# Seven products instead of eight for ten gate/up chunks of one row block, with sums and a load placed elsewhere

## The chip, the cores and the metric

The kernel runs on one core of a Trainium2 chip. A core has a matrix engine (TensorE, PE in the profile), three engines for element work (VectorE, DVE; ScalarE, ACT; GpSimd, POOL) and queues for DMA (most transfers here are issued by SyncE, SP). Each engine works through its own instructions in order and waits for others at semaphores. Matrix products land in PSUM, in banks of 512 f32 values per partition; PE and ACT, DVE and PE hand such banks to each other. POOL works on SBUF only in this kernel. The metric is device time in microseconds (us); lower is better.

## The reference

```python
xn = _layernorm(x, axis=-1)                      # x: 2048 x 512
s = _A_ref(xn, A_k_cache, A_v_cache, A_wq, A_wo) # 32 heads, 2048 keys, Dh 128
g = _silu(_B_ref(xn, B_W_gate, B_W_up, B_W_down))
return x + s * g

def _B_ref(x, W_gate, W_up, W_down):             # D 512, F 1792
    gate = jnp.einsum("bsd,df->bsf", x, W_gate)
    up = jnp.einsum("bsd,df->bsf", x, W_up)
    gate = gate * (gate > 0)
    return jnp.einsum("bsf,fd->bsd", gate * up, W_down)
```

The change concerns gate and up of `_B_ref` for one quarter of the rows.

## The kernel before, in words

The 2048 rows are four blocks of 512 (Q = 0 to 3); the 1792 hidden columns are 14 chunks of 128 (fc). PE runs one long program in the order in which the code emits it, and the time before and after the attention's main loop is one stream: block 0's gate/up, its down products, block 2's gate/up, then the attention of 32 heads, into which the rest of the gated unit (blocks 1 and 3, and down for blocks 1 to 3) is mixed piece by piece.

**Block 0.** `head_ln` and `emit_gate_up(0)` (L715) give gate and up from centered rows. Chunk by chunk: four matmuls into a gate bank (L739), four into an up bank (L743), then `finish_gate_up` (L693): ACT takes relu of the gate bank (L699), DVE multiplies with the up bank into hT (L703). Banks come from a ring of three slots of two banks (`ring_acquire`), or are the two banks of ps_acc. After each chunk `ln_task` (L571) does a step of the normalization of all rows: statistics on DVE, a square root on ACT, the normalized rows xn_sb on POOL (L455), then a DMA transpose into xnT (L567). These run per quarter of the rows: four POOL instructions and four transposes each.

**Down products of block 0.** `emit_down` (L829) has four tiles of 14 matmuls (L842), in turn in the two banks of ps_acc. Each is gated: tanh on ACT (L850), then on DVE a TENSOR_SCALAR (L854) and a product with the bank into g_sb (L858), which frees the bank for the tile after next.

**Block 2.** `emit_gate_up(2)` goes through 14 chunks as for block 0, with xnT in place of the centered rows. Between the chunks it emits other work:

- `emit_tx` (L599), eight sums on DVE of the halves of xnT into TX, which overwrites xn_sb and so waits for all transposes (L609 to L617). All later products by halves read TX;
- `emit_wd_scale` (L775, the down weights times a constant, DVE) and `emit_wd_sums` (L780, four sums of the down weights, POOL, L789 to L795);
- `emit_sw(0)` (L656), scaling of the first query weights on ACT and four sums on POOL (L677 to L682);
- `emit_st`, the query products of the first two heads (L924), combined on DVE (L929, with one copy, L938);
- the first three score pairs S0 to S2 (L1626), whose exponentials (L1638) start the attention;
- `emit_hs` (L803), sums of the halves of hT on DVE (L813 to L822), read by the down products of block 2 (`emit_d`, L1239, combined at L1248).

All these "products by halves" follow one scheme: a product of 2 x 2 blocks is made from seven products of sums of blocks instead of eight of the blocks themselves, and the results are added up from PSUM by DVE. In the kernel before, the queries, the down products of blocks 1 to 3 and gate/up of blocks 1 and 3 are made so; gate/up of block 2 is not.

Of the kernel before, what the change touches and what calls it, by code (L numbers as in the profile page):

```python
# [52 lines left out]
def bass_recurrent_scan__mha_block_cached__glu_gated_reglu__prompt_kernel(  # L53
# [63 lines left out]
    with ExitStack() as es:  # L117
# [111 lines left out]

        sem_x = [newsem(16) for _ in range(QB)]  # L230
# [36 lines left out]
        sem_fo = newsem()  # L267
        sem_ft = [[newsem(16) for _ in range(2)] for _ in range(QB - 1)]
# [91 lines left out]
        sem_wd.sig(sp.dma_start(Wd_sb[:], B_W_down.rearrange("(c p) d -> p c d", p=128)))  # L360
# [210 lines left out]
        def ln_task(i):  # L571
            if i < 4 * (QB - 1):
# [4 lines left out]
                if i == 2:  # L577
                    ctok = ln_finish(0)
                    _wait(dve, ctok)
# [76 lines left out]
        def emit_sw(pr):  # L656
# [8 lines left out]
            if pr in (0, 2):  # L665
# [49 lines left out]
        def emit_gate_up(Q):  # L715
            qs = slice(Q * NQ, (Q + 1) * NQ)
            h_tok = None
            for fc in range(FC):
                fs = slice(fc * 128, (fc + 1) * 128)
                if Q == 0 and fc < HFC:  # L720
                    s = half_slots[fc]
                    finish_gate_up(Q, fc, s, half_tok[(fc, 0)], half_tok[(fc, 1)])
                    continue
                if Q == 0 and fc == HFC:
# [5 lines left out]
                if fc == 0:  # L730
                    _wait_all(pe, xt_ready[Q])
                xT, xs = (xcT, slice(0, NQ)) if Q == 0 else (xnT, qs)
                if Q == 0 and fc in FCS:
# [4 lines left out]
                for c in range(DC):  # L738
                    ins = pe.matmul(g_ps, Wg_sb[:, c, fs], xT[:, c, xs],  # L739
                                    start=(c == 0), stop=(c == DC - 1))  # L740
                gtok = sem_gate.sig(ins)
                for c in range(DC):
                    ins = pe.matmul(u_ps, Wu_sb[:, c, fs], xT[:, c, xs],  # L743
                                    start=(c == 0), stop=(c == DC - 1))
                gu_tok = sem_gu.sig(ins)
                h_tok = finish_gate_up(Q, fc, s, gtok, gu_tok)
                if Q == 2:
                    if fc < 4:
                        emit_tx(2 * fc)
                        emit_tx(2 * fc + 1)  # L750
                    elif fc < 6:
                        emit_wd_scale(fc - 4)
                    if fc == 3:
                        emit_sw(0)
                    if fc == 5:
                        for k in range(4):
                            emit_wd_sums(k)
                    if fc in (7, 9):
                        gu_scale((fc - 7) // 2)
                    if 9 <= fc < 12:  # L760
                        emit_M([(emit_st, 2, 0, 0, fc - 9)])
                    elif fc == 12:
                        emit_S_pair(0)
                        emit_M([(emit_st, 1, 0, 0, 3)])
                    elif fc == 13:
                        emit_S_pair(1)
                        emit_M([(emit_st, 2, 0, 1, 0)])
                        emit_S_pair(2)
                        for k in range(4):
                            emit_hs(2, 0, k)  # L770
# [9 lines left out]
        def emit_wd_sums(k):  # L780
# [18 lines left out]
            wd_tok["t"] = t  # L799
# [3 lines left out]
        def emit_hs(Q, part, i):  # L803
# [6 lines left out]
            if i == 0:  # L810
                _wait(dve, h_done[(Q, FC - 1 if part else HF + 3)])
                _wait(dve, d_done.get(Q - 2))
                t = dve.tensor_tensor(s3, a11, a21, ALU.subtract)  # L813
# [15 lines left out]
        def emit_down(Q, h_last_tok):  # L829
            assert Q == 0  # L830
            ytok = None
            for j in range(4):
# [28 lines left out]
                acc_free[jb] = gtok  # L861
            y_last["t"] = ytok

# [3 lines left out]
        emit_down(0, emit_gate_up(0))  # L867
# [1306 lines left out]
```

## Time and profile before

| | |
|---|---|
| median of 3 runs | 1237.11 us (1236.94 to 1237.14) |
| profiled execution | 1237.32 us, of it span 1236.0 us |
| granted TensorE clock | 0.999 |
| block 0, gate/up | 0 to 31.5 us |
| block 0, down | 31.5 to 43.6 us |
| block 2, gate/up, with the head of the attention mixed in from 60.85 | 43.6 to 71.4 us |
| attention | from 68.6 us (first score pair) to the end |

The profile is of one execution. Its rows by stage give the length, then for each engine the busy time and the number of instructions. In a timeline row the first number is the start, the second how long the group took, then engine, line, operation, tile written, tiles read, shapes and count, and in brackets how long the engine had been idle and for whom it waited. Instructions of one engine overlap a little: of matmuls in a row each starts before the one ahead has ended, so durations per instruction are read from starts. The rows by group give the busy total, the mean of one in ns, and the idle time ahead of them.

### The profile page before, as it was taken

What the parts mean: (1) busy time and instruction counts of PE and PEld (TensorE: products, weight loads), DVE (VectorE), ACT (ScalarE), POOL (GpSimd) and SP (SyncE); (2) the same over time, 40 slices, a digit from 0 to 9 for tenths busy, and PEclk for the clock granted to TensorE, in tenths of its full rate; (3) what the DMA queues carried; (4) which work ended last, traced back from release to release, by engine and by line L of the source; (5) the groups of instructions that cost most, each with busy time, mean ns of one, the idle gap of its engine ahead of it and who ended that gap; (6) DMA issues with size and microseconds to landing.
All of it is one profiled execution on the core that took longest, in us unless ns stands there. A gap on an engine that the chain in (4) does not pass through costs nothing.

```text
span 1236.0 us, 29081 instructions
## 1 busy us (share of the span) xinstructions
PE 1219.0 (99%) x11717; PEld 817.2 (66%) x11927; DVE 877.4 (71%) x1324; ACT 1041.5 (84%) x1110; POOL 835.1 (68%) x946
## 2 busy tenths in 40 slices
PE   9999999999999999999999999999999999999998
PEld 5466666776666666666666666666666666666665
DVE  6668787667676767677676767676676767675587
ACT  3457877668889999999999999999999999989994
POOL 3355876313767867787688776986778767668368
PEclk9999999999999999999999999999999999999999
DMA  9712331323222544264614653374524472248616
GB/s 276 158 31 37 77 78 26 52 48 94 53 53 52 141 128 122 49 158 109 174 36 120 142 159 89 84 172 100 154 52 120 113 192 48 53 103 162 126 35 141
DMA packets 285061, 127.21 MB, mean 103 GB/s; under 512 B 253696, under 2 KB 279552, under 8 KB 280064
## 3 DMA queue, kind: packets, MB, share of 16 engines
q1 hardware_dynamic: 283584, 124.55, 43.6%
q8 instruction: 95, 1.56, 0.5%
q10 hardware_dynamic: 1344, 0.79, 0.2%
q14 instruction: 38, 0.31, 0.1%
HBM read 57.93 MB, written 25.17 MB: 67 GB/s over the span
## 4 chain that ended last, share of the span: by engine, by line
PE 96%; ACT 2%; issue 1%; DMA 0%; DVE 0%; SPq 0%
PE ps_acc L1735 37%; PE ps_r L1626 34%; PE ps_r L1060 5%; PE ps_r L1178 3%; PE ps_r L1523 3%; PE ps_r L1239 3%; PE ps_r L924 2%; ACT PT L1638 2%; PE ps_r L743 2%; PE ps_r L739 2%; PE ps_r L1458 2%; PE ps_acc L842 1%; PE ps_r L1767 1%; PE ps_r L1555 1%; PE ps_r L1554 1%
## 5 line engine op out<-in xcount | busy, mean ns | idle before, releaser
L1638 ACT ACTIVATE PT<-ps_r 128x1024 bf16<-128x1024 f32 x1024 | 989.8, 1025 | 128.3 <-PE ps_r L1626 114.1
L1735 PEld LDWEIGHTS ps_acc<-V_sb,PT 128*128 128x128 bf16 x8192 | 545.3, 98 | 226.8 <-issue 28.3
L1735 PE MATMUL ps_acc<-V_sb,PT 128*128 128x129 bf16 x8192 | 630.8, 220 | 1.0
L1626 PE MATMUL ps_r<-QT_sb,KT_sb 128*128 128x512 bf16 x1849 | 555.0, 379 | 10.1 <-ACT PT L1638 0.3
L1065 DVE TENSOR_TENSOR UVR<-UVR,ps_r 128x512 f32<-128x512 f32 (+1 forms) x228 | 168.7, 755 | 78.9 <-PE ps_r L1060 76.5
L1626 PEld LDWEIGHTS ps_r<-QT_sb,KT_sb 128*128 128x128 bf16 x2048 | 163.2, 98 | 30.9 <-ACT PT L1638 1.5
L1389 DVE TENSOR_TENSOR s_acc<-s_acc,ps_r 128x1024 f32<-128x1024 f32 x108 | 131.2, 1219 | 36.4 <-PE ps_r L1555 15.0
L1405 DVE TENSOR_TENSOR s_acc<-s_acc,ps_r 128x512 f32<-128x512 f32 x152 | 101.4, 686 | 26.6 <-PE ps_r L1523 21.4
L1658 DVE TENSOR_TENSOR Onorm<-ps_acc,rz_sb 128x512 bf16<-128x512 f32 x127 | 87.8, 691 | 4.4
L1489 POOL TENSOR_TENSOR TI<-OX 128x512 f16<-128x512 f16 x38 | 43.1, 1156 | 69.7 <-issue 68.1
L1655 DVE RECIPROCAL rz_sb<-ps_acc 128x4 f32<-128x4 f32 x127 | 23.2, 183 | 93.6 <-PE ps_acc L1735 92.7
L1025 POOL TENSOR_TENSOR TI<-xn_sb 128x512 f16<-128x512 f16 x48 | 55.8, 1163 | 38.9 <-PE ps_r L1060 38.9
L1065 DVE TENSOR_TENSOR QT_sb<-UVR,ps_r 128x512 bf16<-128x512 f32 x72 | 49.4, 686 | 37.1 <-PE ps_r L1060 34.8
L1489 POOL TENSOR_TENSOR TI<-OT_store 128x512 f16<-128x512 bf16 (+1 forms) x38 | 43.4, 1165 | 32.4 <-PE ps_r L1523 16.1
L1333 POOL TENSOR_TENSOR WX<-Wo_sb 128x512 f16<-128x512 bf16 x7 | 8.1, 1155 | 84.2 <-DVE Wo_sb L1323 45.3
L1025 POOL TENSOR_TENSOR TI<-xn_sb,TI 128x512 f16<-128x512 f16 x48 | 56.0, 1166 | 0.0
L1025 POOL TENSOR_TENSOR TI<-xnT 128x512 f16<-128x512 bf16 x36 | 41.6, 1157 | 13.8 <-PE ps_r L1060 13.8
L1060 PE MATMUL ps_r<-TI,SI 128*128 128x512 f16 x126 | 47.8, 379 | 0.1
L1523 PE MATMUL ps_r<-TI,SI 128*128 128x512 f16 x114 | 43.2, 379 | 0.0
L1025 POOL TENSOR_TENSOR TI<-xnT,TI 128x512 f16<-128x512 bf16 x36 | 41.6, 1156 | 0.0
L1154 POOL TENSOR_SCALAR gB<-gB 128x512 bf16<-128x512 bf16 x14 | 20.8, 1486 | 30.3 <-DVE gB L1184 30.3
L1133 POOL TENSOR_TENSOR UVR<-UVR,UVR 128x512 f32<-128x512 f32 x24 | 29.8, 1274 | 11.3 <-DVE UVR L1065 11.3
(236 smaller groups left out, 1436.5 us busy)
## 6 DMA issues: line engine op xcount, KB each, us to landing
sums<-s_acc SPq DMA_DIRECT2D x20, 1024.0 KB, 4.5
s_acc<-sums SPq DMA_DIRECT2D x18, 1024.0 KB, 6.2
V_sb<-in_A_v_cache_dram SPq DMA_DIRECT2D x32, 512.0 KB, 4.3
Wq_sb<-in_A_wq_dram SPq DMA_DIRECT2D x16, 256.0 KB, 3.5
Wo_sb<-in_A_wo_dram SPq DMA_DIRECT2D x8, 512.0 KB, 3.8
out_dram<-g_sb SPq DMA_DIRECT2D x4, 512.0 KB, 4.5
KR<-sums SPq DMA_DIRECT2D x4, 512.0 KB, 4.5
OT_store<-Onorm SPq DMA_TRANSPOSE x127, 2.7
```

Of the source, the lines that this page charges most:

```text
L1025: return sem_ui.sig(pool.tensor_tensor(dst, x, y, o))
L1060: return sem_up.sig(pe.matmul(dst, lhs, rhs, start=start, stop=stop, skip_group_check=True))
L1065: dve.tensor_tensor(dst, x, ps, ALU.add))
L1178: ins = pe.matmul(ps_r[:, bank, :], L(i), R(i), start=(i == 0), stop=(i == HC - 1))
L1389: t = sem_opa.sig(dve.tensor_tensor(dst, dst, sb, op))
L1405: t = dve.tensor_tensor(dst, dst, sb, op)
L1489: return sem_oi.sig(pool.tensor_tensor(dst, x, y, o))
L1523: return sem_op.sig(pe.matmul(dst, lhs, rhs, start=start, stop=stop, skip_group_check=True))
L1626: ins = pe.matmul(ps_r[:, 2 * s + tt, :], KT_sb[h % 2][:, t * 128:(t + 1) * 128], QT_sb[qt_slot[(h, Q)]][:], start=True, stop=True)
L1638: act.activation(PT[pb][:], ps_r[:, 2 * s:2 * s + 2, :], ACTF.Exp, scale=scale / WSC)
L1658: dve.tensor_tensor(Onorm[ob][:], o_ap, rz_sb[:].to_broadcast([128, 4, Dh]), ALU.mult))
L1735: ins = pe.matmul(o_ap, PT[pb][:, tt, j * 128:(j + 1) * 128], V_sb[vb][:, t, 0:VW], start=(t == 0 and j % 2 == 0), stop=(t == KT - 1 and j ...
```

## The change

Gate/up of block 2 gets a function of its own. Chunks 0 to 9 are taken in five pairs (t = 0 to 4). For a pair, gate and up weights of 256 columns, halved along the 512 inputs, are the four blocks of one factor; the 512 rows, halved along rows and inputs, are those of the other. Seven products (m) of four matmuls each, 128x256, fill one bank with both chunks. Products 1, 6, 7 and 4 of a pair accumulate in one bank, which ACT copies out after 1, 6 and 7; DVE adds the copies to the banks of products 2, 5 and 3. Half of h comes from DVE, half from POOL (`high`). Chunks 10 to 13 (F10 to F13) stay as they were, cut into pieces that stand between products. The order of products and pieces is a table of slots.

```diff
+        def sgu_scale(t, i):
+            W = (Wg_sb, Wu_sb)[i][:, :, 256 * t:256 * (t + 1)]
+            _wait(act, up0_tok[2 * t + 1])
+            f_tok[("w", t)] = sem_fs.sig(act.activation(W, W, ACTF.Copy, scale=GSC))
+        def sgu_sums(t):
...
+            _wait(pool, f_tok[("w", t)])
+            if t >= 3:
+                _wait(pool, y_last["t"])
+            k = f_tok[("x", t, 0)] = sem_fw.sig(pool.tensor_tensor(X[:, 0], a21, a22, ALU.add))
...
+        def sgu_rows():
...
+            _wait_all(dve, xt_ready[2])
+            k = sem_fx.sig(dve.tensor_tensor(XS[0], b12, b11, ALU.subtract))
...
+                if fc in (6, 7):
+                    sgu_scale(0, fc - 6)
+                if fc == 7:
+                    sgu_sums(0)
+                if fc in (9, 10):
+                    sgu_scale(1, fc - 9)
...
+            A = [ps_acc[:, 0, :], ps_acc[:, 1, :], bk(2 * X)]
+            a_free = [[acc_free[0]], [acc_free[1]], None]
...
+                if m == 1:
+                    _wait_all(pe, [f_tok[("w", t)]] + (ring_tok[X] if t == 2 else a_free[t % 3]) + xt_ready[2])
...
+                elif m == 5:
+                    _wait_all(dve, [p, f_tok[("w1", t)], f_tok.get(("hi", t - 2))])
...
+            def high(t):
+                b = t % 2
+                _wait(act, f_tok[("gh", t)])
+                k = sem_fa.sig(act.activation(hgh[b][:], hgh[b][:], ACTF.Relu))
+                _wait_all(pool, [k, f_tok[("uh", t)]])
+                f_tok[("hi", t)] = f_tok["hi"] = sem_fh.sig(pool.tensor_tensor(
...
+            slots = {7 * t + d: (t, m) for t in range(NSP) for m, d in ((1, 0), (6, 4), (2, 6), (7, 8), (5, 10), (4, 12), (3, 16))}
...
+                if n == 7 * (NSP - 1) + 2:
+                    emit_sw(0)
+                if n == e + 5:
+                    emit_wd_scale(0)
+                if n == e + 9:
+                    emit_wd_scale(1)
+            ring_order[:] = [X, Y, Z]
+            for k in range(4):
+                emit_wd_sums(k)
+            gu_scale(0)
+            emit_M([(emit_st, 2, 0, 0, 0)])
...
         def emit_down(Q, h_last_tok):
+            for i in range(2):
+                sgu_scale(2, i)
...
+                if j < 2:
+                    for i in range(2):
+                        sgu_scale(3 + j, i)
+                    sgu_sums(1 + j)
+                if j == 0:
+                    sgu_rows()
+                for k in {1: range(5), 2: (5,), 3: (6, 7)}.get(j, ()):
+                    emit_tx(k)
             y_last["t"] = ytok
+            sgu_sums(3)
+            sgu_sums(4)
```

The load of the down weights moves from the end of the first loads to a place behind the first four transposes (in `ln_task`). `emit_sw(0)` scales on DVE instead of ACT, and the first copy of each query product of the first two heads goes from DVE to ACT. The down products of block 2 wait for the sums of the down weights one by one, no longer for all four.

Three places in the order of instructions. **DVE, gating of block 0's down tiles**, before (sig_sb and g_sb are the gating of the four tiles, hT the first chunk of block 2, xn_sb the sums of emit_tx):

```order
L854 TENSOR_SCALAR sig_sb_66<-sig_sb_66,r_51_68 128x512
L858 TENSOR_TENSOR g_sb<-sig_sb_66,ps_acc 128x512
L854 TENSOR_SCALAR sig_sb_67<-sig_sb_67,r_51_68 128x512
L858 TENSOR_TENSOR g_sb<-sig_sb_67,ps_acc 128x512
L854 TENSOR_SCALAR sig_sb_66<-sig_sb_66,r_51_68 128x512
L858 TENSOR_TENSOR g_sb<-sig_sb_66,ps_acc 128x512
L854 TENSOR_SCALAR sig_sb_67<-sig_sb_67,r_51_68 128x512
L858 TENSOR_TENSOR g_sb<-sig_sb_67,ps_acc 128x512
L703 TENSOR_TENSOR hT_53<-gr_sb_63,ps_r 128x512
L609 TENSOR_TENSOR xn_sb<-xnT 128x2x512
```

and on DVE with the change, from the first tile's gating on (PT holds the row sums of `sgu_rows`):

```order
L1023 TENSOR_SCALAR sig_sb_66<-sig_sb_66,r_51_68 128x512
L1027 TENSOR_TENSOR g_sb<-sig_sb_66,ps_acc 128x512
L762 TENSOR_TENSOR PT<-xnT 128x512
L764 TENSOR_TENSOR PT<-xnT,PT 128x512
L765 TENSOR_TENSOR PT<-xnT 128x512
L767 TENSOR_TENSOR PT<-xnT,PT 128x512
L1023 TENSOR_SCALAR sig_sb_67<-sig_sb_67,r_51_68 128x512
L1027 TENSOR_TENSOR g_sb<-sig_sb_67,ps_acc 128x512
L626 TENSOR_TENSOR xn_sb<-xnT 128x2x512
L628 TENSOR_TENSOR xn_sb<-xnT 128x2x512
L631 TENSOR_TENSOR xn_sb<-xnT,xn_sb 128x2x512
L634 TENSOR_TENSOR xn_sb<-xnT,xn_sb 128x2x512
```

Four row sums stand between the gating of the first and the second tile, and emit_tx, which came behind the last, follows the second.

**POOL, from the normalization on**, before (SW are sums of the first query weights, WdT and Wd those of the down weights):

```order
L455 TENSOR_SCALAR xn_sb<-x_sb_56,rstd_72,nmr_74 128x512 x16
L677 TENSOR_TENSOR SW_68_85<-Wq_sb 128x256
L678 TENSOR_TENSOR SW_68_85<-Wq_sb 128x256
L680 TENSOR_TENSOR SW_68_85<-SW_68_85,Wq_sb 128x256
L682 TENSOR_TENSOR SW_68_85<-Wq_sb,SW_68_85 128x256
L789 TENSOR_TENSOR WdT_57<-Wd_sb_54 128x1792
```

and on POOL with the change, from the last sum of pair 0 on (HW are the weight sums, one number for each pair):

```order
L755 TENSOR_TENSOR HW_155<-Wg_sb_61,HW_155 128x512
L471 TENSOR_SCALAR xn_sb<-x_sb_56,rstd_72,nmr_74 128x512 x8
L750 TENSOR_TENSOR HW_156<-Wu_sb_62 128x512
L752 TENSOR_TENSOR HW_156<-HW_156,Wg_sb_61 128x512
L753 TENSOR_TENSOR HW_156<-Wg_sb_61,Wu_sb_62 128x512
L755 TENSOR_TENSOR HW_156<-Wg_sb_61,HW_156 128x512
L750 TENSOR_TENSOR HW_157<-Wu_sb_62 128x512
```

Sums of pair 0 stand ahead of the last eight normalizations, those of the next two pairs right behind them, and those of the last two, which wait for the last down tile, follow. What comes behind these on POOL with the change (hT is the half of h that POOL makes):

```order
L895 TENSOR_TENSOR hT_53<-hgh_154,huh_152 128x2x256
L697 TENSOR_TENSOR SW_68_85<-Wq_sb 128x256
L698 TENSOR_TENSOR SW_68_85<-Wq_sb 128x256
L700 TENSOR_TENSOR SW_68_85<-SW_68_85,Wq_sb 128x256
L702 TENSOR_TENSOR SW_68_85<-Wq_sb,SW_68_85 128x256
L895 TENSOR_TENSOR hT_53<-hgh_153,huh_151 128x2x256
L895 TENSOR_TENSOR hT_53<-hgh_154,huh_152 128x2x256
L895 TENSOR_TENSOR hT_53<-hgh_153,huh_151 128x2x256
L955 TENSOR_TENSOR WdT_57<-Wd_sb_54 128x1792
```

The query weights' sums stand between the second and the third of POOL's products, and the sums of the down weights behind the fifth.

**PE, behind the down tiles**, before:

```order
L842 MATMUL ps_acc<-Wd_sb_54,hT_34_51 128x512 x56
L739 MATMUL ps_r<-xnT,Wg_sb_61 128x512 x4
L743 MATMUL ps_r<-xnT,Wu_sb_62 128x512 x4
L739 MATMUL ps_r<-xnT,Wg_sb_61 128x512 x4
L743 MATMUL ps_r<-xnT,Wu_sb_62 128x512 x4
```

and on PE with the change (L816 are pieces of F10, L854 products):

```order
L1011 MATMUL ps_acc<-Wd_sb_54,hT_34_51 128x512 x56
L854 MATMUL ps_acc<-xnT,Wg_sb_61 128x256 x4
L816 MATMUL ps_r<-xnT,Wg_sb_61 128x512 x4
L816 MATMUL ps_r<-xnT,Wu_sb_62 128x512 x2
L854 MATMUL ps_acc<-PT,HW_155 128x256 x4
L854 MATMUL ps_r<-xnT,Wg_sb_61 128x256 x4
L854 MATMUL ps_acc<-xnT,Wg_sb_61 128x256 x4
```

The first product behind the down tiles goes into ps_acc, whose banks the tiles used, where the first chunk went into the ring.

More of the change, by code (lines that the diff above doesn't have):

```diff
@@ L745, in emit_gate_up @@
[L745 to L770, printed above, removed]
+                    ins = pe.matmul(u_ps, Wu_sb[:, c, fs], xcT[:, c, :], start=(c == 0), stop=(c == DC - 1))
```

193 lines of the change are left out of this document (169 added, 24 removed).

## The prediction, made before the result was known

> **What bounds the kernel now.** I read the page first, then the waits of TensorE, then the busy time by stage.
>
> ```profile
> PE 1219.0 (99%) x11717; PEld 817.2 (66%) x11927; DVE 877.4 (71%) x1324; ACT 1041.5 (84%) x1110; POOL 835.1 (68%) x946
> PE 96%; ACT 2%; issue 1%; DMA 0%; DVE 0%; SPq 0%
> ```
> ```profile
> PE ps_r L1626 <- ACT PT L1638: 0.3, 1, 0.3
> ```
> ```profile
> 31.50:43.60 12.10, 11.99 (x56) 5.47 (x57) 4.44 (x10) 3.30 (x4) 3.03 (x4) 1.00 0.54 97
> 43.60:60.85 17.25, 17.20 (x80) 7.83 (x80) 14.14 (x21) 8.52 (x14) 7.45 (x5) 1.00 0.96 213
> 60.85:74.40 13.55, 13.49 (x68) 6.13 (x68) 10.55 (x17) 6.41 (x9) 10.91 (x4) 1.00 0.07 16
> ```
>
> TensorE (PE) makes 96% of the chain that ends last, and of its waits on other engines behind the start this 0.3 us is all. The rows by stage have length, then busy time of PE, weight load, DVE, ACT, POOL, then the granted clock. The first is the down products of the first row block, the others gate/up of the third. PE is full in all three, so the time moves by two things alone: PE's own work, and waits that appear in it. DVE and POOL are half idle in the first row, which is where the change puts work.
>
> **The change part by part.**
>
> **Matmuls.**
>
> ```profile
> 85.41 1.69 PE L1239 MATMUL ps_r<-WdT,HS_sb 128*128 128x256 f16 x14
> 86.94 1.69 PE L1239 MATMUL ps_r<-WdT,hT 128*128 128x256 f16 x14
> ```
>
> The row of 43.60:60.85 has 80 matmuls of 512 columns in 17.25 us, 0.216 each; fourteen of 256 take 86.94 - 85.41 = 1.53, 0.109 each. Ten chunks had 80 of the first kind, 17.25 us. Now five pairs of chunks have 7 products of 4 matmuls, 140 x 0.109 = 15.3 us. **-2.0 us**, and this is all that the change can gain.
>
> **Sums beside sums.** Four row sums (L762 to L767) and the eight sums of emit_tx now stand on DVE among the gating of the down tiles, and POOL makes the weight sums of pairs two and three at that time. DVE's sums read two SBUF operands, and so do POOL's. How that goes shows elsewhere:
>
> ```profile
> 436.55 0.68 DVE L1357 TENSOR_TENSOR OX<-OT_store 128x1024 f16<-128x1024 f16 x1
> 445.37 1.36 DVE L1357 TENSOR_TENSOR OX<-OT_store 128x1024 f16<-128x1024 f16 x1
> 1199.71 5.62 DVE L1587 SCALAR_TENSOR_TENSOR s_acc<-s_acc,gT 128x512 f32<-128x512 f32 x4
> ```
> ```profile
> 445.02 1.16 POOL L1025 TENSOR_TENSOR TI<-xnT 128x512 f16<-128x512 bf16 x1
> 446.13 0.87 POOL L1025 TENSOR_TENSOR SI<-Wq_sb 128x128 f16<-128x128 bf16 x1
> 1200.04 1.61 POOL L1591 TENSOR_TENSOR hlT<-s_acc,xT 128x512 bf16<-128x512 f32 x1
> 1201.61 1.60 POOL L1592 TENSOR_TENSOR s_acc<-s_acc,xT 128x512 f32<-128x512 f32 x1
> ```
>
> Alone the DVE sum takes 0.68. At 445.37 POOL's runs until 446.18; DVE's ends at 446.73, 0.55 later: it waited for the whole POOL instruction. From 1199.7 on four of DVE and POOL's take turns, and each POOL start is 1.57 behind the last. So a sum of DVE's that meets a busy POOL costs 0.55 of its own (0.27 with half the elements) plus 1.02 of POOL's.
>
> ```profile
> 31.94 3.03 POOL L455 TENSOR_SCALAR xn_sb<-x_sb,rstd,nmr 128x512 bf16<-128x512 bf16 x4 [2.87 <-DVE nmr L449]
> 31.45 1.28 ACT L850 ACT_TABLE_LOAD   x1
> 34.72 0.69 ACT L850 ACTIVATE sig_sb<-ps_acc,r2h 128x512 f32<-128x512 f32 x1 [1.99 <-PE ps_acc L842]
> 35.97 0.69 DVE L858 TENSOR_TENSOR g_sb<-sig_sb,ps_acc 128x512 bf16<-128x512 f32 x1
> 31.50 12.25 PE L842 MATMUL ps_acc<-Wd_sb,hT 128*128 128x512 bf16 x54
> 46.23 0.69 DVE L609 TENSOR_TENSOR xn_sb<-xnT 128x1024 f16<-128x1024 bf16 x1
> 46.84 0.69 DVE L611 TENSOR_TENSOR xn_sb<-xnT 128x1024 f16<-128x1024 bf16 x1
> ```
> ```profile
> L636 ACT ACTIVATE W<-W 128x1024 bf16<-128x1024 bf16 x14 | 14.7, 1051 | 1.4 <-DMA W<-in_B_W_up_dram 1.4
> L1333 POOL TENSOR_TENSOR WX<-Wo_sb 128x512 f16<-128x512 bf16 x7 | 8.1, 1155 | 84.2 <-DVE Wo_sb L1323 45.3 <-DVE dbuf L1248 38.9
> ```
>
> The POOL row of L1333 prices one weight sum, 1.16, some 1.1 in a queue. POOL's last normalization ended at 34.97; the first pair's four sums now stand ahead of the two last, which puts its end near 36, and the eight sums of pairs two and three follow at once. ACT has two scalings (1.05 each by L636's row) ahead of its table load, and the first gating ends at about 37.4 instead of 36.66. That alone is hidden: the third tile needs its bank at 31.50 + 28 x 0.216 = 37.55. Behind it the four row sums take turns with POOL, 4 x 1.29 = 5.2, to 42.6; two steps of gating (0.49 and 0.69, perhaps one more turn) end at about 44.2. The fourth tile wanted that bank at 31.50 + 42 x 0.216 = 40.57: **a wait of 3.6**. It runs its 3.0 to 47.2.
>
> Next on DVE are five sums of emit_tx, ahead of the third tile's gating. Two meet the last weight sums (3.1), two go freely (1.3, the pace of L609 and L611), and then POOL, released by the fourth tile, starts pair four's sums and the fifth takes a turn (1.6). With the gating, 1.2 and perhaps a turn, that bank is free at about 51.6. The first product (0,1) goes into just this bank, ps_acc[0], where the old code took a ring bank: **4.4 more**. Bounds of the two waits together: 0.9 if nothing contends (37.4, 1.6 of row sums, 1.2, five sums of 0.63, 1.2: 44.5 against 43.6), and 10 if every sum and both gatings wait a turn. I take **+8.0**, since the rows of 1199.7 are the nearest case.
>
> A page has one point more. The Trainium skill, "GPSIMD Engine Reference", 1. Specifications, says POOL contends with DVE instructions in a 2-port mode too, not with those of two SBUF operands alone; by that the gating's TENSOR_SCALAR would wait both times, and the sum would be up to 1 us above mine. No row here shows an f32 TENSOR_SCALAR beside a POOL sum.
>
> **Inside the pairs** DVE still has three sums and a gating when the products start, so its first additions are late for F10's bank: +0.7 (0 to 2).
>
> **The end of the pairs.**
>
> ```profile
> 66.84 0.68 DVE L929 TENSOR_TENSOR QT_sb<-cuv,ps_r 128x512 bf16<-128x512 f32 x1
> 67.44 0.68 DVE L929 TENSOR_TENSOR cuv<-cuv,ps_r 128x512 f32<-128x512 f32 x1
> 53.69 1.25 DVE L778 TENSOR_SCALAR Wd_sb<-Wd_sb 128x3584 bf16<-128x3584 bf16 x1
> 53.32 0.67 POOL L677 TENSOR_TENSOR SW<-Wq_sb 128x256 f16<-128x256 bf16 x1 [18.34 <-DVE xn_sb L617]
> ```
>
> The addition for product (4,5) must wait until POOL has multiplied pair three's chunks, high(2). POOL has ahead of that four sums of Wq (0.67 each), whose scaling on DVE comes only behind product (2,3). From the end of (2,3): 0.8 to its addition, 0.5 scaling, 2.7 sums, 1.2 product of POOL, 5.2 in all; (4,5) ends 8 x 0.436 = 3.5 behind (2,3). DVE starts 1.7 late, and has twelve operations of 0.60 (pace of the L929 rows) and two scalings of the down weights (1.2 each) until the second score pair S1 can have its bank: 1.7 + 7.2 + 2.4 = 11.3. PE's work over the same stretch is nine units of 0.436, two of four matmuls from 512 columns for F13, three for the head, and the two small ones: 9.1. That is 2.2, and 0.5 at the pair S4 behind it: **+2.7** (0 if the scalings fall into gaps, 4.5 if they meet POOL).
>
> **Half sums of h beside the down-weight sums.**
>
> ```profile
> 57.52 3.58 POOL L789 TENSOR_TENSOR WdT<-Wd_sb 128x1792 f16<-128x1792 bf16 x1
> 68.26 3.58 POOL L795 TENSOR_TENSOR WdT<-WdT,Wd_sb 128x1792 f16<-128x1792 f16 x1
> 73.85 0.69 DVE L813 TENSOR_TENSOR HS_sb<-hT 128x1024 f16<-128x1024 f16 x1
> 77.69 0.69 DVE L1248 TENSOR_TENSOR dbuf<-dbuf,ps_r 128x512 f32<-128x512 f32 x1 [0.97 <-PE ps_r L1239]
> 79.26 1.03 PE L924 MATMUL ps_r<-xn_sb,SW 128*128 128x512 f16 x4
> ```
>
> POOL's four sums of the down weights ended at 71.8, ahead of DVE's first half sum at 73.85. Now they start only behind the second scaling, which has moved to the end of the pairs. From there to the first half sum DVE has nine operations of 0.60 and waits some 2 us for the head's products, about 8 us: two POOL sums are done, two of 3.45 are left, and half sums two and three wait for one each, 6.9. DVE had 0.97 idle ahead of L1248, and from its end (78.38) to the products that need its bank (79.26) is 0.9: 6.9 - 1.0 - 0.9 = **+5.0** (0 to 7).
>
> **Clock.**
>
> ```profile
> 1230.00:1236.00 6.00, 2.10 (x13) 0.81 (x10) 2.77 (x4) 0.59 (x1) 3.23 (x3) 0.84 0.72 207
> 1231.70 0.40 PE L1795 MATMUL ps_r<-ident,gT 128*128 128x128 bf16 x4
> 0.76 4.00 PE L485 MATMUL ps_r<-const-bfloat16-1.0 128*128 128x256 bf16 x18 [0.76 <-PEq L2159]
> ```
>
> A mean of 0.84 over six us is half clock for 1.9, so it fell about 2 us behind the last matmul (1232.1). At the start, eighteen matmuls of 256 columns take 4.0, 0.22 each, twice the warm time, so a fall costs some 2 us. Two of the three long waits are followed by PE waiting on DVE again, which hides most of it: **+1.5** (0 to 6). The Trainium skill, "TensorE: Matmul & The Clock Gate", Part 1, asks for an idle window of 3.4 us before the clock halves and a busy one to restore it; an estimate by it is 3 x 1.7 = 5 if nothing hides it. Here less idle time was enough.
>
> Costed at nothing: the copies of products from PSUM, three and a relu per pair, on an ACT that is busy 8.52 of 17.25 in that stage (if they were late, PE would wait for them at every second product). For the later load of the down weights:
>
> ```profile
> 12.15 1.42 SPq L360 DMA_DIRECT2D Wd_sb<-in_B_W_down_dram  x1
> 15.87 5.86 SPq L567 DMA_TRANSPOSE xnT<-xn_sb  x1
> 21.78 1.37 SPq L567 DMA_TRANSPOSE xnT<-xn_sb  x1
> ```
> ```profile
> Wd_sb<-in_B_W_down_dram SPq DMA_DIRECT2D x1, 1792.0 KB, 14.0
> ```
>
> It goes out behind four transposes, of 1.4 each. The first was held 5.9 by the loads ahead, this one the largest; without it, it should be gone by 17 and the load start near 22. It took 14.0 to land, behind loads still on their way; with those gone I take half, 29, ahead of its use at 31.5. At the full 14 it would be 36, the third rival.
>
> **Sum** against the profiled execution (span 1236.0, time 1237.32, that is 1.3 around it): -2.0 + 8.0 + 0.7 + 2.7 + 5.0 + 1.5 = +15.9, 1253.2. The median of the runs is 0.2 lower: **1253.0**.
>
> **The rivals.**
>
> *Turns cost PE nothing.* If DVE's sums went ahead of POOL's in each case, POOL would lose 0.55 per sum, and pair four's weights, used 11 us behind the first product, would bear it. For it: at 1199.7 PE stayed full through the turns. Against it: 445.37, and there DVE's sums gated no bank. Then -2.0 + 0.9 + 0.7 + 2.7 = +2.3 at most, and with the last two hidden too, -1.1: 1236 to 1239.4, not slower. It decides if a sum of DVE's loses less than 0.3 to POOL.
>
> *One of the two meetings only.* Either the half sums come behind POOL's, or the row sums ahead of them: 1240 to 1247.
>
> *The load is late.* If the first transpose is held as long as before, or the load takes its full 14, it lands near 35, and PE waits 3 us at 31.5, some of it instead of the wait at 40.57: 1254 to 1258.
>
> **How the numbers follow.** Forecast (1247 to 1260) 0.60; one meeting 0.14; late load 0.06; turns cost nothing 0.17, mostly inside 0.2%; beyond either end 0.03. A measurement of this kernel tells 0.2%, 2.5 us, from no change; the largest gain of 2.0 is under that, so faster has 0.02, same 0.17, slower 0.81. The 8 in 10 range takes in the forecast, one meeting, the late load and the top of the last rival: 1238 to 1261.
>
> **What would show it.** PE waiting at the fourth down tile and ahead of the first product, for DVE L1027; the row sums (L762 to L767) and emit_tx at 1 us and more each; half sums (L980 to L989) of 3 us and more beside POOL's L955 to L961; products at 0.109 per matmul; granted clock below 1.00 behind 40 us. It is wrong if DVE's sums keep 0.4 and 0.69 with POOL busy, or if PE's busy share from 40 to 100 us stays full.

## The result, and the profile after

The changed kernel takes **1253.11 us** (median of 4 runs, 1252.91 to 1253.81), the kernel before 1237.05 beside it: ratio 1.013, 95% interval 1.0118 to 1.0142, so 16 us slower. The prediction had 1253.0. The sum was right to 0.1 us, its terms less so. The profiled execution took 1253.81, with a span of 1251.3; so 2.5 us of it lie outside the span, against 1.3 before, and the rows below account for the span alone.

The page's busy times, and its chain of work that ended last by engine:

```profile
PE 1221.3 (98%) x11777; PEld 823.0 (66%) x11987; DVE 899.1 (72%) x1337; ACT 1055.6 (84%) x1131; POOL 866.3 (69%) x971
PE 91%; DVE 4%; ACT 3%; issue 2%; POOL 0%; DMA 0%; DVEq 0%; POOLq 0%; ACTq 0%
```

TensorE's share of the chain fell from 96% to 91%, and DVE, which had none, has 4%. Busy times by stage, two rows of the kernel before that the prediction has not shown, then the same stages after (length, busy time of PE, weight load, DVE, ACT and POOL, granted clock, DMA):

```profile
74.40:102.31 27.91, 27.65 (x268) 21.34 (x273) 18.97 (x31) 19.86 (x23) 13.81 (x17) 1.00 0.13 27
102.31:1236.00 1133.69, 1118.63 (x11056) 759.53 (x11253) 807.10 (x1192) 990.74 (x1037) 789.93 (x896) 1.00 0.43 100
```
```profile
31.16:50.05 18.89, 14.07 (x55) 5.64 (x56) 15.30 (x20) 10.62 (x14) 14.84 (x15) 0.91 0.93 160
50.05:72.78 22.73, 21.06 (x164) 15.76 (x166) 20.28 (x29) 11.61 (x22) 17.02 (x16) 1.00 0.31 83
72.78:84.18 11.40, 8.67 (x44) 3.69 (x46) 8.50 (x13) 7.88 (x11) 10.09 (x4) 1.00 0.40 69
84.18:117.14 32.96, 29.19 (x269) 21.86 (x273) 24.43 (x31) 19.60 (x23) 19.67 (x19) 0.95 0.03 6
117.14:1251.30 1134.16, 1118.94 (x11056) 759.64 (x11253) 808.78 (x1192) 990.84 (x1037) 791.17 (x896) 1.00 0.42 99
```

Each row ends where TensorE starts the next stage: the first product by halves (50.05), step 0 of the head's query products (72.78), the down products of block 2 (84.18), the first product behind all of it (117.14, in the kernel before at 102.31). Chunks 10 to 13, 1.725 us each (17.25 / 10), lie in another row now and are taken out here:

| stretch | before | after | difference | predicted |
|---|---|---|---|---|
| to the first down product | 31.50 | 31.16 | -0.3 | 0 |
| down products of block 0 | 12.10 | 18.89 | **+6.8** | +8.0 |
| chunks 0 to 9 (after: 22.73 less three chunks) | 17.25 | 17.55 | +0.3 | -2.0 + 0.7 |
| head of the attention (less four chunks, less one) | 6.65 | 9.67 | **+3.0** | +2.7 |
| down products of block 2 | 27.91 | 32.96 | **+5.1** | +5.0 |
| the rest | 1133.69 | 1134.16 | +0.5 | 0 |
| clock, in the rows above | | | | +1.5 |

The differences sum to 15.3, that of the spans. Where TensorE waited (its timeline, the main waits of each row; start, length, and in brackets the wait ahead of the row):

```profile
38.09 3.19 PE L1011 MATMUL ps_acc<-Wd_sb,hT 128*128 128x512 bf16 x14 [0.72 <-DVE g_sb L1027]
44.56 4.77 PE L1011 MATMUL ps_acc<-Wd_sb,hT 128*128 128x512 bf16 x13 [3.27 <-DVE g_sb L1027]
50.05 0.60 PE L854 MATMUL ps_acc<-xnT,Wg_sb 128*128 128x256 bf16 x4 [0.72 <-issue]
57.06 0.60 PE L854 MATMUL ps_r<-xnT,Wg_sb 128*128 128x256 bf16 x4 [0.54 <-DVE hT L723]
70.63 0.60 PE L854 MATMUL ps_r<-xnT,HW 128*128 128x256 bf16 x4 [0.33 <-DVE huh L875]
80.67 0.60 PE L1811 MATMUL ps_r<-QT_sb,KT_sb 128*128 128x512 bf16 x2 [1.38 <-DVE QT_sb L1108]
92.67 1.89 PE L1103 MATMUL ps_r<-xn_sb,SW 128*128 128x512 f16 x4 [3.51 <-DVE dbuf L1431]
```

All of those shown hang on DVE: "issue" at 50.05 too, since the gating that frees its bank (49.27 below) ends just ahead of it. DVE and POOL during the down products:

```profile
36.12 1.20 DVE L1023 TENSOR_SCALAR sig_sb<-sig_sb,r 128x512 f32<-128x512 f32 x1 [2.73 <-ACT sig_sb L1019]
38.64 1.26 DVE L764 TENSOR_TENSOR PT<-xnT,PT 128x512 f16<-128x512 bf16 x1
42.42 1.37 DVE L1023 TENSOR_SCALAR sig_sb<-sig_sb,r 128x512 f32<-128x512 f32 x1
45.27 1.63 DVE L628 TENSOR_TENSOR xn_sb<-xnT 128x1024 f16<-128x1024 bf16 x1
46.83 0.68 DVE L631 TENSOR_TENSOR xn_sb<-xnT,xn_sb 128x1024 f16<-128x1024 bf16 x1
48.75 0.48 DVE L1023 TENSOR_SCALAR sig_sb<-sig_sb,r 128x512 f32<-128x512 f32 x1
49.27 0.69 DVE L1027 TENSOR_TENSOR g_sb<-sig_sb,ps_acc 128x512 bf16<-128x512 f32 x1
```
```profile
44.76 1.59 POOL L755 TENSOR_TENSOR HW<-Wg_sb,HW 128x512 f16<-128x512 bf16 x1
49.49 1.15 POOL L750 TENSOR_TENSOR HW<-Wu_sb 128x512 f16<-128x512 bf16 x1 [3.13 <-PE ps_acc L1011]
```

The same L1023 takes 0.48 at 48.75, where POOL waits (its 3.13 until 49.49), and 1.20 and 1.37 beside POOL's sums, one of which took 1.59 in place of 1.15; a sum of 1024 elements takes 0.68 and 1.63. The last such place, half sums beside the down-weight sums:

```profile
83.52 3.07 DVE L980 TENSOR_TENSOR HS_sb<-hT 128x1024 f16<-128x1024 f16 x1
86.62 3.95 DVE L983 TENSOR_TENSOR hT<-hT 128x1024 f16<-128x1024 f16 x1
90.60 0.69 DVE L986 TENSOR_TENSOR HS_sb<-hT 128x1024 f16<-128x1024 f16 x1
```
```profile
82.44 3.59 POOL L959 TENSOR_TENSOR Wd<-Wd_sb 128x1792 f16<-128x1792 bf16 x1
85.98 4.04 POOL L961 TENSOR_TENSOR WdT<-WdT,Wd_sb 128x1792 f16<-128x1792 f16 x1
```

L980 ends 0.56 behind L959 and L983 0.55 behind L961, the prediction's 0.55. Behind each of the two long waits the clock was down for one stretch of 3.41 us (stage rows once more, PE's busy time and the clock are what counts):

```profile
40.97:44.37 3.40, 0.32 (x2) 0.00 (x0) 3.37 (x4) 0.69 (x1) 3.32 (x3) 1.00 0.79 174
44.38:47.78 3.40, 3.21 (x8) 1.19 (x9) 3.37 (x5) 0.00 (x0) 1.98 (x2) 0.50 1.15 249
88.75:92.15 3.40, 0.41 (x2) 0.00 (x0) 3.33 (x4) 0.00 (x0) 1.27 (x1) 1.00 0.00 0
92.17:95.57 3.40, 2.90 (x13) 1.59 (x14) 3.13 (x6) 2.92 (x4) 0.00 (x0) 0.50 0.00 0
```

At half clock, half of the time that TensorE worked in such a stretch is lost: 3.21 / 2 = 1.6 us of the +6.8 and 2.90 / 2 = 1.4 of the +5.1 are clock.

### The profile page after: what moved, and what is told of

Read it like the earlier page. It is cut to its first block, busy times and chain, and to the rows that moved or that the text cites. A ratio compares the mean times of both kernels' runs of the same rounds, so it can differ in the third digit from the quotient of the medians.

```text
span 1251.3 us, 29301 instructions
## 1 busy us (share of the span) xinstructions
PE 1221.3 (98%) x11777; PEld 823.0 (66%) x11987; DVE 899.1 (72%) x1337; ACT 1055.6 (84%) x1131; POOL 866.3 (69%) x971
## 3 DMA queue, kind: packets, MB, share of 16 engines
q8 instruction: 95, 1.56, 0.5%
## 4 chain that ended last, share of the span: by engine, by line
PE 91%; DVE 4%; ACT 3%; issue 2%; POOL 0%; DMA 0%; DVEq 0%; POOLq 0%; ACTq 0%
PE ps_acc L1920 36%; PE ps_r L1811 34%; PE ps_r L1243 5%; PE ps_r L1361 3%; PE ps_r L1708 3%; PE ps_r L1422 2%; PE ps_r L1103 2%; ACT PT L1823 2%; PE ps_r L1643 2%; PE ps_r L1952 1%; PE ps_r L1740 1%; PE ps_r L1739 1%; DVE stats L445 0%; PE ps_r L854 0%; DVE sig_sb L1023 0%
## 5 line engine op out<-in xcount | busy, mean ns | idle before, releaser
L1811 PE MATMUL ps_r<-QT_sb,KT_sb 128*128 128x512 bf16 x1849 | 555.2, 379 | 11.8 <-DVE QT_sb L1108 1.7
```

Source lines behind the costliest of these rows:

```text
L1811: ins = pe.matmul(ps_r[:, 2 * s + tt, :], KT_sb[h % 2][:, t * 128:(t + 1) * 128], QT_sb[qt_slot[(h, Q)]][:], start=True, stop=True)
```

## The experiments

The theory: DVE and POOL take turns on sums with two SBUF operands, DVE comes late with banks, TensorE waits, and its clock falls. The rivals are that DVE's order or amount of work does it without POOL, and that each wait has a price of its own. All runs are edits of the changed kernel, but for one of the kernel before. The start of the first product behind the stage ("end of the stage": 117.14 after, 102.31 before) is given beside the time, since behind it nothing was changed. It comes from one profiled execution, the time from all runs.

### POOL's sums of pairs 1 and 2 with one operand

```diff
+            if t in (1, 2):
+                for i, a in enumerate((a21, a11, a12, a22)):
+                    f_tok[("x", t, i)] = sem_fw.sig(pool.tensor_scalar(X[:, i], a, 1.0, None, op0=ALU.mult))
+                return
```

> POOL's eight sums for pairs 1 and 2 are replaced by eight instructions of the same size that read one operand each, so the weight sums of these two pairs, and h of their chunks, are left out. The order on DVE and POOL is unchanged. Theory (DVE and POOL take turns on sums with two SBUF operands): the four row sums (L762 to L767) fall from 0.66, 1.26, 1.38 and 1.37 us to about 0.4 each, the gating beside them (L1023) from 1.20 and 1.37 to 0.49, the second gating ends near 40.2 instead of 44.5, the fourth down tile (44.56) starts near 41 with no wait over 0.3, and the clock fall at 44.4 goes. Most of it comes back ahead of the first product: five sums of emit_tx stand ahead of the third gating, cannot start before the last transpose (issued at 40.0, landing 3.0 later) and meet POOL's sums of pair 3, so that product starts between 47.4 and 49 instead of 50.05: 1250.5 to 1252. Rival (DVE's sums are slow there for another reason, the transposes and loads of that time): row sums stay at 1.3, the wait of 3.3 stays, 1253.

1251.56 us (ratio 1.012, 1.0105 to 1.0135); end of the stage 115.61. TensorE's fourth tile and first product, and a row of DVE and of POOL:

```profile
41.11 3.20 PE L1015 MATMUL ps_acc<-Wd_sb,hT 128*128 128x512 bf16 x13 [0.21 <-DVE g_sb L1031]
48.16 1.01 PE L858 MATMUL ps_acc<-xnT,Wg_sb 128*128 128x256 bf16 x4 [3.86 <-issue]
```
```profile
38.77 0.42 DVE L769 TENSOR_TENSOR PT<-xnT 128x512 f16<-128x512 bf16 x1
43.67 3.39 POOL L752 TENSOR_SCALAR HW<-Wg_sb 128x512 f16<-128x512 bf16 x2
```

The weight sums of these pairs, and so h of their chunks, are left out. The wait of 3.27 became 0.21 and came back as 3.86 ahead of the first product, at 48.16 as expected. That DVE's sums are slow of themselves falls. But the stage, from 31.34 to 48.16, is still 16.8 us long, against 18.9 with the change and 12.1 before: with the order kept, 2.1 of the 6.8 us go. What is left comes from the order on DVE, which waits for the last transpose until 42.43 and then makes five sums of emit_tx, of 0.68 to 1.10 beside POOL's one-operand instructions, ahead of the third gating; POOL's sums of pair 3 begin only at 48.65 and have no part in it. POOL's one-operand instructions took 1.5 to 1.7 each and slowed half of the row sums a little (0.82, against 0.42 for the others).

### The row sums behind the second gating; emit_tx behind the last

```diff
-                if j == 0:
+                if j == 1:
                     sgu_rows()
```

> The four row sums are moved from behind the first gating to behind the second, still ahead of emit_tx. Theory (what counts is all of DVE's work, with its turns, ahead of the third gating; a wait only shows where a bank is next wanted): the second gating ends near 41 and the fourth tile waits at most 0.5, but row sums and five sums of emit_tx then stand ahead of the third gating, which ends between 49.5 and 51.5, and the first product waits 5 to 7 us in place of 0.7. The time stays within 1.5 us of the change: 1252 to 1254. Rival (each wait has a price of its own): the 3.3 us and the clock fall behind it go, about 1248.

```diff
-                for k in {1: range(5), 2: (5,), 3: (6, 7)}.get(j, ()):
+                for k in {3: range(8)}.get(j, ()):
                     emit_tx(k)
```

> All eight sums of emit_tx come behind the fourth gating instead of between gatings two and four. Theory: the wait of 3.3 at the fourth tile stays, the third gating ends ahead of the fourth tile, and the wait of 0.7 ahead of the first product goes; then eight sums beside POOL's sums of pairs 3 and 4 take turns, about 1.45 us each, so DVE's first additions of the pairs come near 64 instead of 55.5 and PE waits 8 to 10 us for the bank of chunk F10 or of a product: 1259 to 1262. Rival (only the order of DVE's work counts, no turns): eight sums of 0.63, additions from 57.7, a wait of 2 to 3: about 1255. Second rival (the place of the sums is of no matter): 1252.5.

1257.79 us (1.0165, 1.0148 to 1.0181; end of the stage 122.38) and 1263.54 (1.0213, 1.0198 to 1.0229; 127.36). The wait of TensorE and one of the sums of emit_tx, in the first and in the second:

```profile
55.45 1.01 PE L854 MATMUL ps_acc<-xnT,Wg_sb 128*128 128x256 bf16 x4 [10.49 <-issue]
47.03 1.63 DVE L628 TENSOR_TENSOR xn_sb<-xnT 128x1024 f16<-128x1024 bf16 x1
```
```profile
64.35 1.01 PE L854 MATMUL ps_r<-xnT,Wg_sb 128*128 128x256 bf16 x4 [8.97 <-DVE hT L723]
57.42 1.63 DVE L626 TENSOR_TENSOR xn_sb<-xnT 128x1024 f16<-128x1024 bf16 x1
```

The rivals fall (1248 for the first, 1255 and 1252.5 for the second): moving the sums costs 4.7 and 10.4 us. The second came 1.5 above its range; the clock was at half from 59.43 to 69.67, half of that behind its wait. The first missed the size by more. Without the wait at tile four that tile ends 4 us sooner, which releases POOL's sums of pairs 3 and 4 sooner, and now all five sums of emit_tx ahead of the third gating take 1.5 to 1.6 where three had run free. In the changed kernel the wait at tile four had kept POOL out of DVE's way. The order decides here by what meets POOL.

### The weight sums of pairs 1 and 2 on DVE

```diff
+            eng, sem = (dve, sem_fw2) if t in (1, 2) else (pool, sem_fw)
...
+                _wait(pool, tx_tok[(1, 3)])
...
+                if j < 2:
+                    sgu_sums(1 + j)
+                if j == 2:
+                    sgu_rows()
                 _wait(dve, stok)
...
+                for k in {2: (0, 1), 3: range(2, 8)}.get(j, ()):
                     emit_tx(k)
```

> The eight weight sums of pairs 1 and 2 go from POOL to DVE: pair 1 ahead of the first gating, where DVE sat idle for 2.73 us, pair 2 ahead of the second; the row sums stand ahead of the third, two sums of emit_tx ahead of the fourth and six behind it. POOL makes the weight sums of pairs 3 and 4 only behind emit_tx, the last two behind its product for pair 1. Theory: with nothing on POOL a weight sum takes DVE 0.4 to 0.45 (the row sums' pace in the run with one operand), a row sum the same, emit_tx 0.63, a gating 1.2; the fourth tile and the first product wait at most 0.5 each in place of 3.27 and 0.72, the clock does not fall at 44, and the first product starts between 43.5 and 45 instead of 50.05. DVE's first additions are some 2.5 late, which costs 0.5 to 1.5 in the pairs. All in all 1246.5 to 1248.5. Rival (the amount of DVE's work ahead of the gating decides, not POOL's): 3.2 us more on DVE make the waits of tile four and the first product longer by up to 3, 1254 to 1256.

1250.11 us (1.0107, 1.0092 to 1.0122); end of the stage 113.36. The first product, the waits left in the pairs, and a weight sum on DVE:

```profile
44.07 0.60 PE L859 MATMUL ps_acc<-xnT,Wg_sb 128*128 128x256 bf16 x4
51.51 0.60 PE L859 MATMUL ps_r<-xnT,Wg_sb 128*128 128x256 bf16 x4 [1.57 <-DVE hT L724]
66.88 0.60 PE L859 MATMUL ps_r<-xnT,HW 128*128 128x256 bf16 x4 [1.78 <-DVE huh L880]
```
```profile
38.67 0.42 DVE L758 TENSOR_TENSOR HW<-Wg_sb,Wu_sb 128x512 f16<-128x512 bf16 x1
```

More work on DVE and, from 37 to 50.24, none on POOL: fourth tile and first product wait for nothing, the product starts at 44.07 instead of 50.05, and a sum that costs POOL 1.15 and DVE a turn costs DVE 0.42. The amount of DVE's work falls as a cause. The edit also moves the row sums and emit_tx behind later gatings, so it does not tell POOL's part from that of the order; no run has this order with the weight sums on POOL. The time is 1.6 above the range, since of the 6.0 us gained by then 2.2 were lost again: the additions of the first pair are late (1.57), and POOL's product for pair 2 stands behind more sums (1.78).

### The down-weight sums in quarters; the half sums first

```diff
+            for q in range(4):
+                d = slice(64 * q, 64 * (q + 1))
...
+                    t = pool.tensor_tensor(WdT[:, 0, :, d], b12[:, :, d], b11[:, :, d], ALU.subtract)
```

> Each of POOL's four sums of the down weights (L955 to L961, 3.58 to 4.04 us) is cut into four of 448 elements. Theory (a DVE sum waits until the POOL instruction that is running has ended): the half sums L980 and L983 fall from 3.07 and 3.95 us to at most 0.69 + 0.97 each, step 1 of the query products no longer waits (3.51 us for DVE's dbuf), the clock fall at 92.2 goes, and 3.5 + 1.4 = 4.9 us are gained: about 1248. Rival (the two share the bandwidth, or the half sums are slow of themselves): L980 and L983 stay at 3 to 4 us, the wait stays, 1253.

```diff
-            for k in range(4):
+            for k in range(2):
                 emit_wd_sums(k)
...
             for k in range(4):
                 emit_hs(2, 0, k)
+            _wait(pool, hs_tok[(2, 0, 3)])
+            for k in range(2, 4):
+                emit_wd_sums(k)
```

> POOL's third and fourth sum of the down weights (L959, L961) wait until the four half sums of h (L980 to L989) are done; nothing else is moved. Theory: the first two end at 82.4, the half sums start at 83.5 and take 0.6 to 0.7 each instead of 3.07 and 3.95, step 1 of the query products does not wait (3.51), the clock does not fall at 92, which is worth 4.9. The half sums of the second part (768 elements) then meet L959 and L961, two waits of up to 3.5, of which DVE's slack hides most: 1248 to 1251. Rival (POOL's work is only put off, and the same wait comes later): 1252.5 to 1253.5.

1250.31 us (1.0111, 1.0096 to 1.0126; end of the stage 114.04) and 1253.13 (1.013, 1.0115 to 1.0145; 115.87). With quarters, and then with the half sums first:

```profile
85.06 1.40 DVE L986 TENSOR_TENSOR hT<-hT 128x1024 f16<-128x1024 f16 x1
89.99 1.04 PE L1106 MATMUL ps_r<-xn_sb,SW 128*128 128x512 f16 x4 [0.66 <-DVE dbuf L1434]
```
```profile
83.94 0.69 DVE L986 TENSOR_TENSOR hT<-hT 128x1024 f16<-128x1024 f16 x1
90.19 3.81 DVE L986 TENSOR_TENSOR hT<-hT 128x768 f16<-128x768 f16 x1
95.44 0.60 PE L1106 MATMUL ps_r<-xnT,SW 128*128 128x512 bf16 x2 [2.72 <-DVE cuv L1111]
```

Quarters bring a half sum to 1.35 to 1.40: a DVE sum waits for the instruction that runs on POOL, whatever that one's length, and not for a share of bandwidth. The gain was 2.8 and not 4.9, since the halves' four sums now met POOL four times (5.5 us in all, against 8.4), where two had met it before. In the second run, with the half sums first, they run free (0.69), but those of the second part meet what was put off (3.81), and TensorE waits 2.72 one product later. The time is the rival's, but the four runs reach from 1251.38 to 1254.89. In the profiled one the row of the down products, from 85.10, is 2.2 shorter (30.8 against 33.0), and 0.9 is lost ahead of it, where the clock was at half for two stretches at tile four and one at 81.02. So the order moved part of the wait; how much time that is worth, these runs do not tell.

### The head of the attention

```diff
-                if n == 7 * (NSP - 1) + 2:
+                if n == 33:
                     emit_sw(0)
```

> The scaling of the first query weights and POOL's four sums of them (L684, L697 to L702) come behind POOL's product for pair 2 instead of ahead of it. Theory: DVE's addition L875 of pair 4 no longer waits 1.37 us for that product, and the waits at the end of the pairs (0.33, 0.26, 0.60, 0.44, 1.38 and 0.29, 3.3 in all) fall to 1.7 to 2.2: 1251.5 to 1252. Rival (these waits come from the count of DVE's operations there, not from the late start): 1253. Second rival: the sums come too late for step 1 of the query products (75.36), 1254 or more.

The other run is the kernel before:

```diff
-                    if 9 <= fc < 12:
-                        emit_M([(emit_st, 2, 0, 0, fc - 9)])
...
+                    if fc == 12:
+                        emit_M([(emit_st, 2, 0, 0, 0)])
+                    elif fc == 13:
+                        emit_M([(emit_st, 2, 0, 0, 1)])
+                        emit_M([(emit_st, 2, 0, 0, 2)])
+                        emit_S_pair(0)
+                        emit_M([(emit_st, 1, 0, 0, 3)])
+                        emit_S_pair(1)
```

> The kernel before, with one edit: the steps of the first query products and the score pairs S0 to S2 stand behind each other as in the changed kernel (step 0 behind chunk 12, then chunk 13, steps 1 and 2, S0, step 3, S1), where the kernel before had a chunk of 1.7 us between one step and the next. No product by halves of gate/up is in it, and no sum is moved. Theory (the last three waits at the end of the pairs, 0.44, 1.38 and 0.29 us, come from this order: steps 1 to 3 give DVE six additions of 0.6 and TensorE only 2.6 us of work): the same waits appear here, 2.1 us, and 0.6 to 1.2 more since this kernel makes its copies on DVE: 1239 to 1240.5. Rival (they come from the pairs, by DVE's backlog or POOL): no wait over 0.3, 1237 to 1237.5.

1252.52 us (1.0123, 1.0106 to 1.014; end of the stage 116.39) and 1238.72 (1.0013, 1.0003 to 1.0022; 10 runs). The first is above its range, the second below. The longest wait of the head in the first, and in the second:

```profile
79.46 0.61 PE L1811 MATMUL ps_r<-QT_sb,KT_sb 128*128 128x512 bf16 x2 [1.38 <-DVE QT_sb L1108]
```
```profile
72.71 0.60 PE L1627 MATMUL ps_r<-QT_sb,KT_sb 128*128 128x512 bf16 x2 [1.38 <-DVE QT_sb L930]
```

With the query weights' sums behind POOL's product for pair 2, three of the six waits at the end of the pairs go; 0.44, 1.38 and 0.29 stay. Those that go are 0.33, 0.26 and 0.60, but 0.21 of the last is a matmul whose record is missing (the run with the half sums first has both, and a wait of 0.39): 1.0 us. The time moved by 0.6, which these runs do not tell from 0. The 1.38 then stands in the kernel before too, once its head has the new order, and costs 1.4 at the end of the stage (103.71); the 0.44 and 0.29 do not. So the end of the pairs is three things: the place of POOL's sums (1.0), steps of the head that follow each other with no chunk between (1.4), and 0.7 that stays open.

### All together

combo1 has DVE's weight sums, the half sums first, the down-weight sums in quarters and the query weights behind; combo3 adds an edit of the order of pair 1's sums and waits for single banks; combo2 adds to combo3 the scaling of the down weights inside the pairs; combo4 is combo3 with another order of the head.

> The weight sums of pairs 1 and 2 on DVE, the half sums ahead of the last two sums of the down weights, these cut into quarters, and the query weights behind POOL's product for pair 2, all four together. Theory: the gains add up, about 5.5 + 4.9 + 1.4: 1240 to 1243. Rival (a wait that goes shows the next one, as with the row sums behind the second gating): 1244 to 1249.

> combo2 without its third edit, so the down weights are scaled where they were. Theory: 0.42 and 1.0 to 1.56 of combo1's waits go, those at the end of the pairs stay at 2.8: 1242 to 1243.5. Rival (the wait of 1.56 only moves to the next bank): 1244 to 1245.

> combo1 with three more edits: two of the four weight sums of pair 1 go behind the first gating; products 1, 2 and 5 wait for the one bank that they overwrite, not for both banks of its slot; the scaling of the down weights is cut in four and stands in pairs 2 to 4, not behind them. combo1 has waits of 0.42, 1.56, 0.34, 0.39, 0.44, 1.38, 0.29 and 0.88 us left, 5.7 in all. Theory (each of them is DVE being late): 0.42 goes by the first edit, 1.0 to 1.56 of 1.56 by the second, 1.3 to 2.2 of the five in the middle by the third: 1239.5 to 1242 against combo1's 1244.5. Rival (DVE's work is only moved, and the scalings meet POOL's sums inside the pairs): new waits there, not below combo3.

> combo3 with the head's order changed: step 0 of the query products fills the gap among the products of pair 4 that chunk 12 filled, chunk 12 stands ahead of step 1, and chunk 13 between step 2 and S0. Theory: combo3's waits of 0.57, 0.39, 0.44, 1.38 and 0.29 (3.1 us) fall to 0.3 to 1.0: 1241 to 1242 against 1243.7. Rival (DVE's work there is the same, and it only waits elsewhere): 1243.5 to 1244.

The central edits of the last three:

```diff
-                    _wait_all(pe, ring_tok[s])
+                    _wait_all(pe, ring_tok[s] if t < 2 else [f_tok[("gl", t - 2)]])
...
+            WDN = (20, 25, 29, 33)
+                if n in WDN:
+                    emit_wd_scale(WDN.index(n))
...
+                elif n == e + 8:
+                    ring_order[:] = [Z, X, Y]
+                    emit_M([(emit_st, 2, 0, 0, 0)])
```

| run | median us | ratio, interval | end of the stage |
|---|---|---|---|
| combo1 | 1244.53 | 1.0058, 1.0043 to 1.0073 | 107.18 |
| combo3 | 1243.72 | 1.005, 1.0033 to 1.0067 | 106.94 |
| combo2 | 1245.52 | 1.0068, 1.0053 to 1.0083 | 109.66 |
| combo4 | 1243.39 | 1.0048, 1.0031 to 1.0065 | 107.29 |

combo1 gets 8.6 us back, of the 11.8 to which the expected gains sum. All four came out above their ranges. From combo1 on each edit removed all or part of the waits that it was made for, and others took their place: the 1.56 in combo1 became 1.19 for another bank in combo3; the scalings inside the pairs met POOL's sums there and gave 2.12 and a fallen clock in combo2; combo4's head waits 1.43, 0.47, 1.01 and 0.30 where combo3's had 0.57, 0.39, 0.44, 1.38 and 0.29:

```profile
63.33 0.60 PE L859 MATMUL ps_acc<-PT,HW 128*128 128x256 f16 x4 [2.12 <-ACT PT L867]
```
```profile
66.67 1.02 PE L821 MATMUL ps_r<-xnT,Wg_sb 128*128 128x512 bf16 x4 [1.43 <-issue]
```

So with the long waits gone nearly all that are left are for DVE, directly or, as the 2.12 does, by way of ACT. That DVE now bounds the stage is argued from this; no run takes work off it. No version beat the kernel before; the best is 6.3 us behind it. Of combo3's 6.5 us, 4.6 are there at the end of the stage. The rest comes behind it, where the programs are the same and no long wait stands; in the spans of the profiled executions it differs by 2.2 us between the combos (1134.2 in combo1, 1136.4 in combo3, against 1133.7 before), and its cause stays open.

## Why the prediction was right

- **Matmuls**, -2.0, and **waits inside the pairs**, +0.7: the row of the pairs shows +0.3 for both. Its waits are 0.49, 0.54, 0.33 and 0.26, and each costs some 0.16 more than the timeline shows, since the last of four matmuls ends 0.16 later (0.60) than the next would have started (0.436). That is 2.3, which leaves -2.0 for the matmuls, as predicted. These waits cost 1.6 more than predicted, and the 0.33 and 0.26 among them the prediction had under the end of the pairs.
- **Down stage**, +8.0: measured 5.2 (0.72, 3.27 and 0.72, and 0.16 for each), and 1.6 of clock. The fourth tile's wait, 3.6, was 3.27. The first product's, 4.4, was 0.72: this is the term that was mis-sized. It let the fourth tile end at 47.2, release POOL's sums of pair 4 then, and the bank come free at 51.6. The tile ran at half clock until 47.78 and ended at 49.3, POOL waited for it, three sums of emit_tx and a whole gating ran free, and the bank was free at 50.0. A wait of 0.72 at the third tile had been costed at nothing: L1023 took 1.20 there. The Trainium skill, "GPSIMD Engine Reference", 1. Specifications, has POOL contend with DVE's 2-port modes too; the trace agrees in that L1023, with one SBUF operand of 512, took 0.48 alone and 1.20 and 1.37 beside POOL's sums. In which mode it ran, no trace shows.
- **End of the pairs**, +2.7: six waits of 3.1 in all (0.33, 0.26, 0.39, 0.44, 1.38, 0.29), of which 1.0 comes from the cause named, POOL's product behind the query weights. Another 1.4 comes from the head's order alone, where the prediction had DVE's late start and its scalings, and 0.7 is open. So less than half of the term came by the way predicted, and that its row shows +3.0 is luck.
- **Half sums**, +5.0: measured 3.6, and 1.4 of clock. The turns were as predicted, but the first half sum came 1.1 us into POOL's third sum, so DVE lost 2.4 and 3.3 there (3.07 and 3.95 less 0.69 each) and not twice 3.45.
- **Clock**, +1.5: 3.0, two falls of one stretch each. Here the errors cancel: the two long terms 2.8 and 1.4 too large, clock 1.5, pairs 1.6 and the rest 0.5 too small. The mechanism was right (DVE and POOL in turns, TensorE late for banks, the clock behind it); that the sum came out to 0.1 us is luck.
- **Load of the down weights**, 0: it was in time, the down products start at 31.16 with no wait.
- Of the rivals, the one by which turns cost TensorE nothing fell by the waits of 3.27 and 3.51, the one with one meeting only by there being both of them, and the late load by the start of the down products.

## What to carry to other kernels

An engine's busy share says nothing of two engines that take turns: price a sum on POOL by what it makes DVE wait as well (1.15 on POOL and about 1 on DVE here, against 0.42 if DVE makes it). Look for what a late engine keeps apart: removing a wait of 3.3 let POOL's next sums begin 3 us sooner and made the next wait 10.5. And a saving of 2 us in matmuls is not had where the 59 instructions that it adds on DVE, ACT and POOL (by the two pages) bring new waits for DVE into a stage in which TensorE was full.

## What the runs showed of the hardware

The granted clock changes on a grid of 3.41 us that does not follow the waits, and it falls without a whole idle stretch. Three stretches of the run with the half sums first (stage rows):

```profile
77.60:81.01 3.41, 1.58 (x7) 0.42 (x6) 3.17 (x5) 1.02 (x1) 3.33 (x2) 1.00 0.90 200
81.02:84.42 3.40, 3.40 (x12) 1.46 (x11) 1.77 (x3) 2.50 (x3) 1.17 (x1) 0.50 0.14 30
```
```profile
91.25:94.66 3.41, 1.48 (x15) 0.74 (x12) 3.34 (x2) 3.06 (x4) 2.33 (x1) 1.00 0.00 0
```

Behind the first, with 1.58 of 3.41 busy, the clock fell; behind the last, with 1.48, it stayed at 1.00. The busy time counts 0.16 too much for each unbroken series of matmuls that ends in a stretch (the modelled ends, as above), two of them in the first stretch and one in the last, which leaves about 1.26 and 1.32. Counted so in the traces of all runs here from 30 to 120 us, an estimate: the clock fell behind each of the 15 stretches with up to 1.28 us and behind none with 1.31 or more. The Trainium skill, "TensorE: Matmul & The Clock Gate", Part 1, gives a free-running window of this length, and the trace agrees. What counts as idle is here a stretch with less than some 1.3 us of matmuls. So the same wait costs by its place on the grid: the 3.27 at tile four cost one stretch at half clock in the changed kernel and two in the run with the half sums first:

```profile
43.47:46.87 3.40, 2.24 (x6) 0.87 (x7) 3.37 (x4) 0.00 (x0) 2.94 (x3) 0.50 1.10 251
46.88:50.28 3.40, 3.40 (x10) 1.20 (x9) 3.33 (x7) 0.00 (x0) 0.00 (x0) 0.50 1.37 231
```

A stretch with 2.24 busy did not restore it; those with 2.90 and 3.21 did. Four runs of a kernel with long waits spread by up to 3.5 us, four of the kernel before by 0.2, though of thirteen others of it two lie 0.5 and 1.5 above their median. The grid may be a reason for the wider spread; no run shows it.
